# Experts of a fused attention and MoE kernel: the order of ScalarE, VectorE and GpSimd taken from the scheduler and given by lists

## Chip, cores and metric

The kernel runs on one core of a Trainium2 chip. The metric is the device time of one execution in microseconds (us). Times below in the profile are counted from the start of the profiled execution's span.

## What is computed

```
x  = attention(q, k, v)               # k and v averaged over 8 rows; 2304 tokens x 512
h  = x @ w_in;  x = (h * cos(h)) @ w_out          # 512 -> 2048 -> 512
P  = exp(x @ w_gate - max)                        # 2304 x 8
for _ in range(8):                                # Sinkhorn: rows, then columns
    P /= P.sum(1) + 1e-9;  P /= P.sum(0) + 1e-9;  P *= N / E
for e in range(8):
    out += P[:, e] * (relu(x @ w1[e]) @ w2[e])    # 512 -> 1024 -> 512
```

All is float32. Each operand of a product is split into a high half (float32r, rounded by ScalarE) and a low half (operand minus high half), and a product is three matmuls: high by high, high by low, low by high.

## The kernel before

The first third (to about 530 us) is attention and the cosine layer, and the change leaves it alone but for its end. The rest is the experts: 16 units (8 experts, two halves of 512 hidden columns each) for each of three pairs of 384-token blocks, 48 steps in all. The loop over `steps` (L990) writes one step after the other.

**First layer.** A step multiplies the pair's x by W1 in a Strassen-like scheme with seven products named P1, P5, P6, P2, P7, P3, P4, for two halves g of the columns: 14 blocks of six matmuls, the letters `a` in the order strings (L973 to L975). Px, py and pv are the PSUM banks that a half runs through. After P1, ScalarE copies px into py (L751), and P6, P7 and P4 add into py. After P5, ScalarE copies pv out (L754); VectorE adds it after P6 (L756) and after P7 (L768, or L794).

**Second layer.** Products of the step before run between the blocks. In the 16 steps of the first pair (plain steps) they are six groups `L` of 24 matmuls (L852), and VectorE adds each into the output (L839). In the other two pairs (Strassen steps) they are three groups `0`, `1`, `2` of four turns each (L869): a turn is two products of six matmuls, the last turn one. VectorE adds after the second turn (L888) and after the third (L892). Step 16, the first Strassen one, runs the plain second layer of step 15 (string `SWAP`).

**Preparation in the first pair.** In each plain step the weights of the next units are read raw, summed on GpSimd into Strassen's pieces (`combine`, L571), split (W1 in `split`, L93; W2 in `cut`, L631), and written to HBM for the later pairs (`w1c`, `w2c`). `w1_pieces` makes seven pieces; `w2_pieces` makes four blocks that the plain second layer uses and four sums that are only written out. Raw W2 tiles lie in `xh5` and `xl5`, raw W1 tiles in a pool of three. W1's halves lie in a pool of 19 tiles, W2's in `wp2` with 18. A tile comes free when its last reader is done, and for the pieces that includes the write to HBM.

**Preparation of x.** `x_pieces` makes seven pieces of the next pair's x in the last step of a pair (steps 15 and 31).

**Gate.** Logits, maximum, exponential and the eight Sinkhorn rounds run in steps 0 and 1. A round is a product with ones for the column sums (L555), then VectorE's scaling (`sinkhorn_columns`) and row and column sums (`sinkhorn_rows`).

**Order.** `tc.manual_schedule` (L976) holds TensorE alone to program order. ScalarE, VectorE, GpSimd and the DMA issues (all on SP's queue) are ordered by the framework's scheduler with its own model of time. `after[k]` is a list of calls that are made behind block k; what they issue on TensorE stands there, the rest is only traced from there.

Of the kernel before, what the change touches and what calls it, by code (L numbers as in the profile page):

```python
# [22 lines left out]
P = 128  # L23
# [35 lines left out]
def fused_kernel(ctx: ExitStack, tc: tile.TileContext, qT, kT, vT, v0, wa1, wb1, wa2, wb2, wg, out):  # L59
# [423 lines left out]
    def open_gate():  # L483

        gc = right(ctx, "gc", 1, reuse_waits="tile")
        gate["sk"] = right(ctx, "sk", 2, reuse_waits="tile")
        gate["tmp"] = right(ctx, "tmp", 3, reuse_waits="tile")
# [16 lines left out]
    def logits(j):  # L504

        sk = gate["sk"]
# [5 lines left out]
        lt = sk.tile([G2 + E, NB], F32, tag="lt", name="lt")  # L512
        nc.vector.tensor_copy(out=lt, in_=ps[:G2 + E, :])
        pq = gate["ps"][0].tile([P, TPB, E], F32, tag=gate["ps"][1], name="pq")
# [4 lines left out]
    def gate_max():  # L519

        sk, lg = gate["sk"], gate["lg"]
        m1 = sk.tile([P, 1], F32, tag="m1", name="m1")
        nc.vector.tensor_reduce(out=m1, in_=lg, op=ALU.max, axis=AX.XY)
        pm = gate["ps"][0].tile([P, P], F32, tag=gate["ps"][1], name="pm")
        nc.tensor.transpose(pm[:1, :], m1, ident)
        m2 = sk.tile([1, 1], F32, tag="m2", name="m2")
# [12 lines left out]
    def sinkhorn_rows():  # L539

        sk, pr = gate["sk"], gate["pr"]
        rw = sk.tile([P, NT, 1], F32, tag="rw", name="rw")
# [3 lines left out]
        nc.vector.tensor_tensor(out=pr, in0=pr, in1=rw.to_broadcast([P, NT, E]), op=ALU.mult)  # L546
        cs = sk.tile([P, E], F32, tag="cs", name="cs")
        nc.vector.tensor_reduce(out=cs, in_=pr.rearrange("p t e -> p e t"), op=ALU.add, axis=AX.X)
        gate["cs"] = cs

    def sinkhorn_columns():

        sk, pr = gate["sk"], gate["pr"]
        pc = gate["ps"][0].tile([P, E], F32, tag=gate["ps"][1], name="pc")
        nc.tensor.matmul(out=pc, lhsT=gate["ones"], rhs=gate["cs"], start=True, stop=True)  # L555
        cr = sk.tile([P, 1, E], F32, tag="cr", name="cr")
        nc.vector.tensor_scalar(
            out=cr[:, 0, :], in0=pc, scalar1=EPS, scalar2=float(E) / T, op0=ALU.add, op1=ALU.mult
        )
        nc.vector.reciprocal(out=cr, in_=cr)  # L560
        nc.vector.tensor_tensor(out=pr, in0=pr, in1=cr.to_broadcast([P, NT, E]), op=ALU.mult)
# [7 lines left out]

    def combine(out, x, y, op):  # L570
        nc.gpsimd.tensor_tensor(out=out, in0=x, in1=y, op=op)  # L571
        return out

    def w1_pieces(u):
# [10 lines left out]
        def piece(name):  # L585
            if name == "P1":
                what = a(1, 1)
            elif name == "P5":
                src["t"] = gate["tmp"].tile([P, FU], F32, tag="s", name="s")
                what = combine(src["t"], a(2, 1), a(2, 2), ALU.add)  # L590
            elif name == "P2":
                what = a(1, 2)
            elif name == "P6":
                what = combine(src["t"], src["t"], a(1, 1), ALU.subtract)
            elif name == "P7":
                what = combine(a(2, 1), a(1, 1), a(2, 1), ALU.subtract)
            elif name == "P3":
                what = combine(a(1, 2), a(1, 2), src["t"], ALU.subtract)
            else:
                what = a(2, 2)  # L600
            parts = split(what, nc.vector)
            for k, part in enumerate(parts):
                nc.sync.dma_start(out=w1c[u, ORDER.index(name), :, :, k, :],
                                  in_=part.bitcast(F32).rearrange("p (g n) -> p g n", g=2))
            w[name] = [[part[:, g * HD:(g + 1) * HD] for part in parts] for g in range(2)]

        return w, [lambda i=i: load(i) for i in range(2)], [lambda n=n: piece(n) for n in ORDER]
# [6 lines left out]
    def w2_pool(name):  # L614
        return wp if name in ("P1", "P5") else gate["wp2"]

    def w2_pieces(u):
# [3 lines left out]
        def load(h):  # L621
            src[h] = xp.tile([P, 2, DM], F32, tag=("xh5", "xl5")[h], name="raw2")
# [8 lines left out]
        def cut(what, pool, lo_engine):  # L631
            hi = pool.tile([P, FU], F32R, tag="w", name="vhi")
            lo = pool.tile([P, FU], F32R, tag="w", name="vlo")
            nc.scalar.activation(out=flat(hi), in_=what, func=AF.Copy)
            lo_engine.tensor_tensor(out=flat(lo), in0=what, in1=flat(hi).bitcast(F32), op=ALU.subtract)  # L635
            return hi, lo

        def keep(name, parts):
            for k, part in enumerate(parts):
                nc.sync.dma_start(out=w2c[u, ORDER.index(name), k], in_=part.bitcast(F32))  # L640

        def block(h, d):
            w[h - 1, d - 1] = cut(b(h, d), gate["wp2"], nc.gpsimd)
            name = {(1, 1): "P1", (2, 1): "P2", (2, 2): "P3"}.get((h, d))
            if name:
                keep(name, w[h - 1, d - 1])

        def tmp():
            return gate["tmp"].tile([P, 2, HD], F32, tag="s", name="t")

        def total(name):
            if name == "P5":
                src["t"] = combine(tmp(), b(1, 2), b(1, 1), ALU.subtract)
                what = src["t"]
            elif name == "P6":
                what = combine(src["t"], b(2, 2), src["t"], ALU.subtract)
            elif name == "P7":
                what = combine(tmp(), b(2, 2), b(1, 2), ALU.subtract)
            else:
                what = combine(src["t"], b(2, 1), src["t"], ALU.subtract)  # L660
            keep(name, cut(what, gate["wp2"], nc.vector))

        todo = [lambda h=h, d=d: block(h, d) for h, d in ((1, 1), (1, 2), (2, 1), (2, 2))]
        todo += [lambda n=n: total(n) for n in ("P5", "P6", "P7", "P4")]
        return w, [lambda h=h: load(h) for h in range(2)], todo

    def w2_cached(u, w, name):
        parts = []
        for k in range(2):
            t = w2_pool(name).tile([P, FU], F32R, tag="w", name="wc2")  # L670
# [6 lines left out]
    def x_pieces(pair):  # L677
# [13 lines left out]
        def piece(name):  # L691
# [4 lines left out]
            if name == "P1":  # L696
                what = b(1, 1)
            elif name == "P5":
                what = b(1, 1)
                nc.gpsimd.tensor_tensor(out=what, in0=b(1, 2), in1=b(1, 1), op=ALU.subtract)  # L700
            elif name == "P2":
                what = b(2, 1)
            elif name == "P6":
                what = b(1, 1)
                nc.gpsimd.tensor_tensor(out=what, in0=b(2, 2), in1=what, op=ALU.subtract)
            elif name == "P7":
                what = b(1, 2)
                nc.gpsimd.tensor_tensor(out=what, in0=b(2, 2), in1=what, op=ALU.subtract)
            elif name == "P3":
                what = b(2, 2)  # L710
            else:
                what = b(2, 1)
                nc.gpsimd.tensor_tensor(out=what, in0=what, in1=b(1, 1), op=ALU.subtract)
            t = xp.tile([P, 2, 2, NB], F32R, tag=XTAGS[name], name="xc")
            nc.scalar.activation(out=t[:, 0], in_=what, func=AF.Copy)
            nc.vector.tensor_tensor(out=t[:, 1], in0=what, in1=t[:, 0].bitcast(F32), op=ALU.subtract)  # L716
            x[name] = (t[:, 0], t[:, 1])

        return x, [lambda j=j: load(j) for j in (1, 2)], [lambda n=n: piece(n) for n in ORDER]

    def g_split(c, g):

        gh, gl = g_tiles(g)
        nc.scalar.activation(out=gh, in_=c, func=AF.Relu)
        nc.vector.scalar_tensor_tensor(
            out=gl, in0=c, scalar=0.0, in1=gh.bitcast(F32), op0=ALU.max, op1=ALU.subtract
        )
        return gh, gl
# [11 lines left out]
    def first_layer(weights, x, result):  # L740

        def sub(g, name, s):
            if name == "P1":
# [4 lines left out]
            ps = s[{"P1": "x", "P2": "x", "P5": "v", "P3": "v"}.get(name, "y")]  # L748
            x_product(ps, weights(name, g), x[name], name in ("P1", "P5"))
            if name == "P1":  # L750
                nc.scalar.activation(out=s["y"], in_=ps, func=AF.Copy)  # L751
            elif name == "P5":
                s["s5"] = cp.tile([P, NB], F32, tag="s5", name="s5", bufs=2)
                nc.scalar.activation(out=s["s5"], in_=ps, func=AF.Copy)  # L754
            elif name == "P6":
                nc.vector.tensor_tensor(out=s["v"], in0=ps, in1=s["s5"], op=ALU.add)  # L756
            else:
# [5 lines left out]
    def plain_result(gs):  # L763

        def result(g, name, ps, s):
            if name == "P7":
                c22 = cp.tile([P, NB], F32, tag="c22", name="c22")
                nc.vector.tensor_tensor(out=c22, in0=ps, in1=s["s5"], op=ALU.add)  # L768
                ps = c22
            h, j = {"P2": (0, 0), "P3": (0, 1), "P7": (1, 1), "P4": (1, 0)}[name]  # L770
            gs[2 * g + h, j] = g_split(ps, g)
# [3 lines left out]
    def strassen_result(pieces):  # L775
# [339 lines left out]
```

## Time and profile before

| | us |
|---|---|
| median of 3 runs | 2041.73 (2037.03 to 2042.55) |
| profiled execution | 2042.21 |
| its span | 2040.5 |
| first product of the experts (TensorE's first block of step 0) | 533.38 |

A row of the timeline names start, length, engine, line, what is written from what, count, and in brackets the idle time before and what ended it. In the windows each engine has its busy time and its number of instructions; then come TensorE's granted clock (1.00 is 2.4 GHz, 0.5 is 1.2 GHz), the mean busy share of the DMA engines and GB/s. A matmul's length in a row holds its latency; how fast they go is read from start to start.

### The profile page before, as it was taken

What the parts mean: (1) busy time and instruction counts of PE and PEld (TensorE: products, weight loads), DVE (VectorE), ACT (ScalarE), POOL (GpSimd) and SP (SyncE); (2) the same over time, 40 slices, a digit from 0 to 9 for tenths busy, and PEclk for the clock granted to TensorE, in tenths of its full rate; (3) what the DMA queues carried; (4) which work ended last, traced back from release to release, by engine and by line L of the source; (5) the groups of instructions that cost most, each with busy time, mean ns of one, the idle gap of its engine ahead of it and who ended that gap; (6) DMA issues with size and microseconds to landing.
All of it is one profiled execution on the core that took longest, in us unless ns stands there. A gap on an engine that the chain in (4) does not pass through costs nothing.

```text
span 2040.5 us, 36395 instructions
## 1 busy us (share of the span) xinstructions
PE 1966.0 (96%) x13220; PEld 1917.3 (94%) x13220; DVE 1380.9 (68%) x2279; ACT 992.3 (49%) x2133; POOL 770.8 (38%) x646
## 2 busy tenths in 40 slices
PE   6799999999889999999999999999999999999999
PEld 4689899999889999999999999999998999999999
DVE  8988776655786555556565676667667666666766
ACT  5676566655544444434443444444445444444443
POOL 7755644433344545454532221222223222222212
PEclk8899999999989999999999999999999999999999
DMA  7433331212688988888896776677677777667763
GB/s 254 144 123 126 113 119 53 84 52 77 228 292 296 304 276 301 270 293 292 278 316 222 266 263 229 240 275 250 225 256 250 241 261 275 230 235 269 258 230 121
DMA packets 257458, 453.32 MB, mean 222 GB/s; under 512 B 25568, under 2 KB 86752, under 8 KB 257280
## 3 DMA queue, kind: packets, MB, share of 16 engines
q1 hardware_dynamic: 257280, 451.01, 64.5%
q8 instruction: 104, 1.70, 0.3%
q14 instruction: 74, 0.61, 0.1%
HBM read 317.21 MB, written 133.69 MB: 221 GB/s over the span
## 4 chain that ended last, share of the span: by engine, by line
PE 76%; DVE 6%; DMA 6%; POOL 4%; ACT 3%; issue 3%; SPq 0%; ACTq 0%; POOLq 0%; DVEq 0%
PE pc L869 13%; PE py L736 13%; PE qc L869 10%; PE po L852 8%; PE px L736 8%; PE pv L736 8%; DMA w2c<-vhi 2%; PE ph L138 2%; PE po L137 2%; PE po L139 2%; PE ph L139 2%; PE po L138 2%; PE ph L137 2%; POOL vlo L635 1%; POOL t L571 1%
## 5 line engine op out<-in xcount | busy, mean ns | idle before, releaser
L869 PE MATMUL pc<-wc,gh 128*128 128x256 f32 x1536 | 284.1, 280 | 0.0
L571 POOL TENSOR_TENSOR sf<-spare 128x384 f32<-128x384 f32 x64 | 65.7, 1027 | 509.9 <-DVE spare L800 509.9
L869 PEld LDWEIGHTS pc<-wc,gh 128*128 128x128 f32 x1536 | 241.1, 188 | 0.0
L736 PE MATMUL py<-xc,wc 128*128 128x384 f32 x1152 | 236.1, 340 | 0.9 <-DVE c L794 0.6
L869 PE MATMUL pc<-wc,gl 128*128 128x256 f32 x768 | 215.6, 281 | 0.0
L869 PE MATMUL qc<-wc,gh 128*128 128x256 f32 x1152 | 214.1, 280 | 1.5 <-DVE pc L888 1.5
L736 PEld LDWEIGHTS py<-xc,wc 128*128 128x128 f32 x1152 | 196.6, 189 | 7.4 <-ACT py L751 5.1
L783 DVE TENSOR_TENSOR gl<-sf,gh 128x384 fp32r<-128x384 f32 x256 | 183.8, 758 | 10.8 <-ACT gh L782 7.3
L869 PEld LDWEIGHTS qc<-wc,gh 128*128 128x128 f32 x1152 | 185.9, 188 | 2.0 <-DVE pc L888 1.8
L869 PE MATMUL qc<-wc,gl 128*128 128x256 f32 x576 | 161.7, 281 | 0.0
L571 POOL TENSOR_TENSOR sf<-sf 128x384 f32<-128x384 f32 x64 | 80.8, 1262 | 210.9 <-DVE gl L783 210.9
L736 PE MATMUL pv<-xc,wc 128*128 128x384 f32 x768 | 156.2, 338 | 3.8 <-DVE xc L716 2.0
L736 PE MATMUL px<-xc,wc 128*128 128x384 f32 x768 | 154.3, 335 | 0.0
L852 PE MATMUL po<-vlo,gh 128*128 128x256 f32 x768 | 153.1, 281 | 0.0
L852 PE MATMUL po<-vhi,gl 128*128 128x256 f32 x768 | 152.8, 281 | 0.0
L852 PE MATMUL po<-vhi,gh 128*128 128x256 f32 x768 | 152.6, 281 | 0.0
L782 ACT ACTIVATE gh<-sf 128x384 fp32r<-128x384 f32 x256 | 119.9, 517 | 52.5 <-POOL sf L571 32.8
L869 PEld LDWEIGHTS pc<-wc,gl 128*128 128x128 f32 x768 | 145.1, 189 | 0.2 <-DVE gl L783 0.2
L137 PE MATMUL ph<-xh,whi 128*128 128x384 f32 x384 | 131.3, 346 | 5.9 <-DVE r L389 5.9
L736 PEld LDWEIGHTS pv<-xc,wc 128*128 128x128 f32 x768 | 131.0, 189 | 4.6 <-DVE xc L716 2.2
L138 PE MATMUL ph<-xl,whi 128*128 128x384 f32 x384 | 131.5, 343 | 0.7 <-DVE xl L370 0.7
L138 PE MATMUL po<-gl,whi 128*128 128x384 f32 x384 | 129.5, 338 | 0.8 <-POOL gl L392 0.8
(203 smaller groups left out, 5136.1 us busy)
## 6 DMA issues: line engine op xcount, KB each, us to landing
wc<-w1c SPq DMA_DIRECT2D x448, 256.0 KB, 5.2
wc<-w2c SPq DMA_DIRECT2D x448, 256.0 KB, 5.4
w1c<-whi SPq DMA_DIRECT2D x112, 256.0 KB, 3.4
w1c<-wlo SPq DMA_DIRECT2D x112, 256.0 KB, 3.3
w2c<-vhi SPq DMA_DIRECT2D x112, 256.0 KB, 3.9
w2c<-vlo SPq DMA_DIRECT2D x112, 256.0 KB, 4.3
raw<-wa SPq DMA_DIRECT2D x48, 512.0 KB, 6.2
raw<-wb SPq DMA_DIRECT2D x48, 512.0 KB, 4.6
```

The source lines that it names most:

```text
L137: nc.tensor.matmul(out=ps, lhsT=lh, rhs=rh, start=(i == 0), stop=False)
L138: nc.tensor.matmul(out=ps, lhsT=lh, rhs=rl, start=False, stop=False)
L139: nc.tensor.matmul(out=ps, lhsT=ll, rhs=rh, start=False, stop=(i == n - 1))
L571: nc.gpsimd.tensor_tensor(out=out, in0=x, in1=y, op=op)
L635: lo_engine.tensor_tensor(out=flat(lo), in0=what, in1=flat(hi).bitcast(F32), op=ALU.subtract)
L736: nc.tensor.matmul(out=ps, lhsT=l[:, k], rhs=r[:, c, :], start=(start and c + n == 0), stop=(c + n == 3), skip_group_check=True)
L782: nc.scalar.activation(out=hi, in_=t, func=AF.Copy)
L783: nc.vector.tensor_tensor(out=lo, in0=t, in1=hi.bitcast(F32), op=ALU.subtract)
L852: nc.tensor.matmul(out=po[:, d * HD:(d + 1) * HD], lhsT=l[:, r], rhs=w[f % 2, d][k][:, (f // 2) * HD:(f // 2 + 1) * HD], start=(f + n + d ...
L869: nc.tensor.matmul(out=ps, lhsT=l[:, r], rhs=m[:, k], start=(start and g + n == 0), stop=(g + n == 3), skip_group_check=True)
```

## The change

In the experts, ScalarE, VectorE and GpSimd too are held to program order:

```
-    with tc.manual_schedule(engines={mybir.EngineType.PE}):
+    E_ = mybir.EngineType
+    with tc.manual_schedule(engines={E_.PE, E_.Activation, E_.DVE, E_.Pool}):
         prime()
+        plan["on"] = True
```

The program order is made by three lists, one for each engine. `later` puts a call on a list, with the slot from which it may be made, its cost in us and a condition. After each block or group `tick` makes calls until the time of that block or group is used up. `until` makes calls ahead of time when a product needs what they give. A call made by `spent` is charged but was issued at once.

```
+    def later(engine, slots, us, run_it, at=0, ready=None, soon=False):
+        if plan["on"]:
+            k = sum(item[4] for item in plan[engine]) if soon else len(plan[engine])
+            plan[engine].insert(k, (max(plan["now"] + slots, at), us, run_it, ready, soon))
+        else:
+            run_it()
+    def tick(us):
+        for engine in "GAV":
+            left = min(plan["left"][engine] + us, max(us, 1.5))
+            k = 0
+            while k < len(plan[engine]) and left > 0:
+                slot, cost, run_it, ready, _ = plan[engine][k]
+                if slot > plan["now"] or (ready and not ready()):
+                    k += 1
+                    continue
+                plan[engine].pop(k)
+                run_it()
+                left -= cost
+            plan["left"][engine] = left
+        plan["now"] += 1
+    def until(done):
+        while not done():
+            ...      # makes the first ready call of each list
+    def parts_of(src, hi, lo, us, then, engine="V", slots=0, at=0):
+        def low():
+            e = nc.gpsimd if engine == "G" else nc.vector
+            e.tensor_tensor(out=lo(), in0=src, in1=high.bitcast(F32), op=ALU.subtract)
+            then()
+        def first():
+            nonlocal high
+            high = hi()
+            nc.scalar.activation(out=high, in_=src, func=AF.Copy)
+            later(engine, 1, us[1], low)
+        high = None
+        later("A", slots, us[0], first, at)
```

The ticks: 1.04 for a block, 2.8 for a plain group, 1.4 for a Strassen turn. Copies, ReLUs and sums that TensorE's next products need are issued at once; low halves, cuts, sums of pieces and gate operations go by the lists. `first_layer`, `plain_layer` and `strassen_layer` call `until` for the pieces that they read.

Engines that change: W1's low halves go from VectorE to GpSimd for units 0 to 2, and W2's low halves of the blocks with d = 2 from GpSimd to VectorE from unit 2 on; x's low halves of P7 and P3 go to GpSimd in the loop.

```
-            parts = split(what, nc.vector)
+            engine = "G" if u < 3 else "V"
+            parts_of(what, ..., (0.63, 1.4 if u < 3 else 0.8), done, engine, 0, at)
-            w[h - 1, d - 1] = cut(b(h, d), gate["wp2"], nc.gpsimd)
+            later("A", 0, 0.0, lambda: cut(..., "G" if d == 1 or u < 2 else "V"), 0, lambda: 1 in src)
+                engine = "G" if plan["on"] and name in ("P7", "P3") else "V"
```

Places in a plain step. W2's sums come ahead of its blocks, raw tiles are asked for from block 12 on, when all cuts of the pair in use are issued, and W2's last raw pair takes the raw W1 pool, so that x of pair 1 can be loaded at block 1 of step 15:

```
-                    put((0, 0), load)
-                    put((1, 3, 5, 7, 8, 9, 10, 11) if not last else (1, 2, 3, 4, 5, 6, 7, 8), todo)
-                    put(range(0, 14, 2), w_todo)
+                    for k, name in zip(((8, 9, 11, 13), (3, 4, 6, 9), (0, 1, 3, 9))[min(n, 2)], ("P5", "P7", "P6", "P4")):
+                        put(k, total, name)
+                    for k, (h, d) in zip((5, 7, 9, 11) if n else (5, 6, 7, 8), ((1, 1), (1, 2), (2, 1), (2, 2))):
+                        put(k, block, h, d)
+                        for k, name in ((3, "P5"), (4, "P6"), (7, "P7"), (8, "P3")):
+                            put(k, nw1[2], name)
+                        for k, name in enumerate(ORDER):
+                            put(5 + k, nw1[3], name)
+                                put(12, later, "A", 0, 0.0, lambda h=h, f=w1_next[1]: f(h), 0, lambda w=nw1[0]: len(w) == 7)
+                            put(12, later, "A", 0, 0.0, lambda h=h, f=w2_now[1]: f(h), 0, w2_read)
-                    put((8, 8) if pair == 0 else (2, 2), x_load)
+                        put(1, later, "A", 0, 0.0, f)
```

The gate's rounds stand three blocks apart in steps 1 and 2, and the output of expert 0 is scaled once the rounds are done (`first_scale`). The order strings change, and Strassen's pieces have 18 tiles of each half, where they had 20 low and 16 high. From step 17 on, the cuts of P7, P6, P2 and P3 of the first half wait for slot 16 of the step:

```
-    rest = [[lambda: logits(GRP[1][1])], [gate_max], [gate_exp, sinkhorn_rows], [], half, [], half]
-    rest += [half] * (SINKHORN_ITERS - 3) + [[sinkhorn_columns]]
+    rest = [{0: [late_logits], 2: [late_turn], 5: [max_turn], 8: [late_exp], 12: half},
+            {k: half for k in (1, 4, 7, 10, 13)}, {2: half, 5: [lambda: columns(False)]}]
-    GB = {"gl": 20, "gh": 16}
-    PLAIN = "aaLaaLaaLaaLaaLaaLaa"
+    GB = 18
+    PLAIN = "aaLaaLaaLaaaLaaLaaLa"
-    STRASSEN = "aaa0a1a01a01a01a2aa2a2a2aa"
+    STRASSEN = "aa0a1a0a1a0a1a0a2a1a2a2a2a"
+            free = start + 16 if g == 0 else 0
```

One pool of small gate tiles goes from 2 to 1 buffer, the pool of sums from 3 to 4, and the plain P3 of the first half takes its tile from the second half's pool.

## Rows read from the trace of the kernel before

**Rows 1.** The page: span, and each engine's busy us, share, instructions.
```profile
span 2040.5 us, 36395 instructions
...
PE 1966.0 (96%) x13220; PEld 1917.3 (94%) x13220; DVE 1380.9 (68%) x2279; ACT 992.3 (49%) x2133; POOL 770.8 (38%) x646
```
**Rows 2.** Windows: steps 0, 1, 2, 3 to 14, 16, 18, 31 to 32.
```profile
533.38:561.47 28.09, 21.71 (x106) 19.66 (x105) 18.11 (x36) 13.14 (x26) 15.09 (x11) 0.88 0.86 292
561.47:606.39 44.92, 36.10 (x241) 34.96 (x241) 39.01 (x85) 17.83 (x35) 19.56 (x15) 0.89 0.81 284
606.39:637.79 31.40, 31.40 (x229) 31.40 (x229) 23.37 (x35) 14.51 (x28) 18.01 (x14) 1.00 0.91 310
637.79:1030.89 393.10, 381.17 (x2737) 376.69 (x2737) 227.90 (x349) 170.24 (x324) 203.44 (x147) 1.00 0.86 288
1062.29:1099.08 36.79, 34.57 (x229) 32.80 (x229) 22.10 (x27) 12.21 (x25) 9.66 (x6) 0.95 0.83 301
1128.75:1158.30 29.55, 29.55 (x212) 29.40 (x211) 19.98 (x32) 13.48 (x33) 6.81 (x7) 1.00 0.70 242
1512.86:1578.26 65.40, 61.48 (x422) 60.07 (x422) 49.19 (x71) 32.42 (x72) 22.78 (x17) 0.97 0.71 239
```
**Rows 3.** Timeline of TensorE: first matmul of a P1 block, a group, a P5 block.
```profile
686.42 0.33 PE L736 MATMUL px<-xh,whi 128*128 128x384 f32 x1
...
687.46 0.40 PE L852 MATMUL po<-vhi,gh 128*128 128x256 f32 x2
...
690.26 0.51 PE L736 MATMUL pv<-xc,whi 128*128 128x384 f32 x2
```
**Rows 4.** Waits of TensorE in steps 0 and 1: total us, times, longest.
```profile
PE pc L555 <- DVE cs L548: 10.6, 4, 7.8
```
**Rows 5.** Waits of TensorE in steps 2 to 14.
```profile
PE py L736 <- ACT py L751: 10.3, 11, 1.7
```
**Rows 6.** Waits of TensorE from 1062 us to the end.
```profile
PE pv L736 <- DVE xc L716: 2.0, 1, 2.0
PE pv L736 <- ACT sf L802: 1.8, 1, 1.8
PE qc L869 <- DVE pc L888: 1.5, 1, 1.5
```
**Rows 7.** Timeline of ScalarE in step 4.
```profile
686.62 0.49 ACT L724 ACTIVATE gh<-py 128x384 fp32r<-128x384 f32 x1
691.33 0.63 ACT L634 ACTIVATE vhi<-t 128x512 fp32r<-128x512 f32 x1 [4.22 <-DMA w2c<-vhi]
691.87 0.61 ACT L96 ACTIVATE whi<-raw 128x512 fp32r<-128x512 f32 x1
692.38 0.47 ACT L751 ACTIVATE py<-px 128x384 f32<-128x384 f32 x1
```
**Rows 8.** Timeline of TensorE: the P6 block behind that copy.
```profile
692.91 0.44 PE L736 MATMUL py<-xc,whi 128*128 128x384 f32 x1 [1.44 <-ACT py L751]
```
**Rows 9.** Lines of GpSimd, steps 0 and 1: busy us, mean ns, idle before.
```profile
L635 POOL TENSOR_TENSOR vlo<-raw,vhi 128x512 fp32r<-128x512 f32 x10 | 14.4, 1462 | 9.1 <-ACT vhi L634 9.1
...
L571 POOL TENSOR_TENSOR t<-raw 128x512 f32<-128x512 f32 x2 | 2.6, 1311 | 2.2 <-DMA raw<-wb 2.2
```
**Rows 10.** Timeline of GpSimd at the loop's start.
```profile
537.66 1.28 POOL L571 TENSOR_TENSOR s<-raw 128x512 f32<-128x512 f32 x1 [20.36 <-DMA raw<-wa]
```
**Rows 11.** The page, DMA issues: count, KB each, median us to landing.
```profile
raw<-wb SPq DMA_DIRECT2D x48, 512.0 KB, 4.6
```
**Rows 12.** Timeline of VectorE in step 22.
```profile
1260.59 0.75 DVE L839 SCALAR_TENSOR_TENSOR acc<-pc,pr,acc 128x512 f32<-128x512 f32 x1 [0.27 <-PE pc L869]
1261.26 1.10 DVE L783 TENSOR_TENSOR gl<-spare,gh 128x384 fp32r<-128x384 f32 x1
...
1266.48 0.56 DVE L783 TENSOR_TENSOR gl<-c,gh 128x384 fp32r<-128x384 f32 x1 [1.28 <-ACT gh L782]
1266.95 2.31 DVE L783 TENSOR_TENSOR gl<-sf,gh 128x384 fp32r<-128x384 f32 x3
...
1270.40 0.43 DVE L888 TENSOR_TENSOR pc<-qc,t 128x256 f32<-128x256 f32 x1
```
**Rows 13.** Timeline of GpSimd in step 22.
```profile
1267.58 1.26 POOL L571 TENSOR_TENSOR sf<-sf 128x384 f32<-128x384 f32 x1 [5.63 <-DVE gl L783]
```
**Rows 14.** Lines of VectorE in steps 3 to 14: the low half of W1.
```profile
L97 DVE TENSOR_TENSOR wlo<-raw,whi 128x512 fp32r<-128x512 f32 x60 | 45.5, 759 | 3.2 <-PE px L736 2.0
```

More of the change, by code (lines that the diff above doesn't have):

```diff
@@ L583, in a, with total, t @@
             return src[i - 1][:, j - 1, :]
[L585 to L592, printed above, removed]
+        def total(name):
+            def t():
+                return gate["tmp"].tile([P, FU], F32, tag="s", name="s")
+            if name == "P5":
+                src["P5"] = combine(t(), a(2, 1), a(2, 2), ALU.add)
@@ L601, in piece @@
-            parts = split(what, nc.vector)
[L602 to L607, printed above, removed]
+                src["P3"] = combine(a(1, 2), a(1, 2), src["P6"], ALU.subtract)
@@ L629, in flat, with keep @@
             return t.rearrange("p (g n) -> p g n", g=2)
[L631 to L640, printed above, removed]
+        def keep(name, k, part):
+            nc.sync.dma_start(out=w2c[u, ORDER.index(name), k], in_=part.bitcast(F32))
@@ new lines, in cut, with tile_of, done @@
+        def cut(what, name, then, engine):
+            got = {}
+            def tile_of(k):
+                got[k] = gate["wp2"].tile([P, FU], F32R, tag="w", name=("vhi", "vlo")[k])
+                return flat(got[k])
+            def done():
+                if name:
+                    for k in range(2):
+                        keep(name, k, got[k])
+                then(got)
+            parts_of(what, lambda: tile_of(0), lambda: tile_of(1), (0.65, 1.4 if engine == "G" else 0.8), done, engine)
@@ L742, in sub @@
         def sub(g, name, s):
+            until(lambda: name in x and weights(name, g) is not None)
+            until(lambda: not any(reads[b] for b in {"P1": "xy", "P5": "v"}.get(name, "")))
             if name == "P1":
@@ L845, in group @@
         def group(j, i):
+            until(lambda: len(w) == 4 and all((f, j) in gs for f in range(FC)))
             po = psp.tile([P, DM], F32, tag="p", name="po")
@@ L863, in mm @@
             r = slice(i * P, (i + 1) * P)
+            until(lambda: all((name, g) in pieces for g in range(2)))
             wh, wl = w[name]
@@ L1026, in fused_kernel @@
-                    nxt = strassen_layer(pair, u, pieces, w2, acc2, own)
-                x_next = x_op
+                    first = first_layer(lambda name, g, n=n: ring[n, name, g], x_op, strassen_result(pieces, start if n > NU else start - 99))
+                    own = {2: ((psx, "x"), (psy, "y"))} if n == len(steps) - 1 else None
+                    nxt = strassen_layer(pair, u, pieces, w2, acc2, own)
+                if n == UE:
+                    for j in range(2):
+                        for i in range(TPB):
+                            put(13, later, "V", 0, 0.65, lambda j=j, i=i, a=acc2: first_scale(j, i, a), 0,
+                                lambda: gate.get("done"))
```

411 lines of the change are left out of this document (261 added, 150 removed).

## The prediction, made before the changed kernel ran

> **What bounds the kernel now.** I read the busy shares first. TensorE is busy 96% of the span and no other engine is above 68% [rows 1], so time can come only from TensorE's gaps and slow stretches. The second view is the windows by expert step [rows 2]. Step 2 is a clean plain step. Its 31.40 us equal 14 first-layer blocks of 1.04 and 6 second-layer groups of 2.80, both read as distances between matmul starts [rows 3]: 14.56 + 16.80 = 31.36. Step 18 is a clean Strassen step of 29.55. Against these two the other windows show what is lost:
>
> - Steps 0 and 1 take 28.09 and 44.92, where 14 blocks (14.6) and a plain step (31.4) would do: 27.0 over. Their counts of 106 and 241 hold 22 and 13 matmuls beyond the 84 and 228 of the products. These 35 small ones are the gate's own; at no more than 0.174 each (1.04 / 6) they explain 6 at most, and I put them at 5. So 22 is lost.
> - Steps 3 to 14 take 393.10, twelve clean ones 376.8: 16.3 lost.
> - Step 16, the passage to Strassen: 36.79 against 31.4: 5.4 lost.
> - Steps 31 and 32, where the last pair's x is prepared: 65.40 against 59.1: 6.3 lost.
>
> Together 50.0 us. Some of it is half speed: the granted clock is 0.88 and 0.89 in the first two windows, which hold TensorE's longest idle stretch, and 1.00 in the clean ones [rows 2].
>
> The third view is TensorE's waits, which name the culprits. In steps 0 and 1 it waited 10.6 for VectorE's column sums, 7.8 of that at once [rows 4]. In steps 2 to 14 it waited 10.3 for ScalarE's copy of px into py, 11 times [rows 5]. After that come single waits of 2.0, 1.8 and 1.5 at the two passages [rows 6]. The fourth view, ScalarE's order of time, shows why the copy is late [rows 7]. It sits behind a cut of W2 whose buffer was still being written to HBM: ScalarE stood 4.22 there, did two cuts, copied at 692.38, and TensorE's P6 began at 692.91 after 1.44 idle [rows 8]. Its input had been ready since 687.46.
>
> **The change, part by part.** No matmul goes or comes. ScalarE, VectorE and GpSimd lose the scheduler's order and run in the order in which the lists emit. Sums are made on the profiled execution's own 2042.2 us (span 2040.5 and 1.7 around it), which is 0.5 above the median of 2041.73.
>
> *Gate rounds (part of steps 0 and 1).* They go from every second block of steps 0 and 1 to every third of steps 1 and 2. Between two column products there are then three blocks and one or two groups, 5.9 to 8.7 us, in place of two blocks and at most one group. A round is some eight small VectorE operations, and 7.8 was lost when they came late. These waits go. What is late next is GpSimd.
>
> *Low halves of W1 on GpSimd for units 0 to 2 (steps 0 to 2).* Each step cuts seven W1 pieces and four W2 blocks and makes eight sums. In steps 0 and 1 the 11 low halves cost 1.46 each on GpSimd and the 8 sums 1.31 [rows 9]: 16.1 + 10.5 = 26.6 us. Unit 0's seven low halves fall ahead of the loop, where GpSimd was idle for 20.36 [rows 10], and cost nothing; without that cover they would cost up to 2. Step 0's work starts when its raw tile lands at 537.7 and ends at 564.3 if nothing holds it. Step 1 would start near 551.5 (533.4 + 14.6 + some 3.5 of the gate). Its first group, two blocks on, needs the last W2 block, which lies eight items before the end, at 553: just in time. The second 26.6 cannot start whole at 564.3, since W2's next raw pair reuses the tiles just read: a last cut of 1.5 and a landing of 4.6 [rows 11] put it at 570. GpSimd ends between 590.9 (W1's share fills the hole) and 597. Step 2's first group (551.5 + 32.9 + 2.1 = 586.5) needs the W2 block that is last but one in that order: 589.4 to 595.5. So TensorE waits 3 to 9 there. VectorE's delays behind so busy a GpSimd add 1 to 8. Of the 22 lost I keep 9 (ends 4 and 17): 13 gained.
>
> Here a row speaks against the change. Three VectorE low halves in a row took 2.31 while one GpSimd product of 1.26 ran beside them [rows 12, 13]; with GpSimd idle the next one followed 0.47 after the first (1266.48 to 1266.95), so among the three one stood about as long as the product. The Trainium skill, SBUF — State Buffer, section "Who interferes with whom", has the rule: a VectorE instruction with two SBUF inputs and a GpSimd instruction that reads SBUF share a port and the later one stands until the first is done. The trace agrees with it. By that rule moving low halves to GpSimd frees VectorE of less than their length; it is a rival below.
>
> *W2's sums ahead of its blocks, raw tiles asked for after the last cut (steps 3 to 14).* The four sums move from blocks 8 to 11 to blocks 0, 1, 3 and 9. At block 0 only the eight W2 tiles of the unit in use are held, of 18. The sums' six tiles find room, and their writes have landed before the blocks need it. So the wait in front of the copy goes [rows 7]. The plain order also puts a group between P5 and P6 of the second half, which gives that copy 2.80 + 1.04 in place of 1.04. Two low halves per step go from GpSimd to VectorE, at 0.76 each [rows 14]; VectorE is busy 228 of 393 there and takes it. New is that ScalarE's first cut of a step stands behind a GpSimd sum, which stands behind a raw tile asked for near the last group of the step before: 4.6 to land, 1.3 for the sum. That is about 6 us, and the cut stands some 6 to 9 us after the request. Queued behind it are the ReLU of P2 and later the copy of P1, which TensorE needs some 9 us on. Five us of lateness stay hidden. Of 16.3 I keep 2.5 (ends 0 and 8): 13.8 gained.
>
> *Step 16.* The x tiles of pair 1 are asked for at block 1 of step 15 in place of 8, since W2's last raw pair moves to another pool, and two of their low halves go to GpSimd. TensorE's 2.0 wait for VectorE's xc goes. The memory that the Strassen tiles reuse still has to be freed at the same point. Of 5.4 I keep 2.4: 3.0 gained.
>
> *Steps 31 and 32.* The same seven pieces, loaded a block earlier, with VectorE at 49.19 of 65.40 busy. Two of seven low halves leave it and the rest come by budget. Of 6.3 I keep 3.0 (ends 0 and 8): 3.3 gained.
>
> *Strassen order (steps 17 to 47).* No row shows a loss here now, so the edit can only cost. Groups 0 and 1 get more room between their turns. Group 2's second and third turn have one block between them as before: VectorE must add (L888) between P6 and the next turn's P7. In the new order P6's block ends 4.2 us before that P7 (a last turn 0.70, a block 1.04, a turn 1.40, a block 1.04). VectorE has the P6 add, up to four low halves that were held for that slot, and one accumulation ahead of the add: 0.47 + 4 x 0.47 + 0.67 + 0.43 = 3.45 alone (starts in [rows 12]). 0.7 is left. Bounds: 0 per step, and 1.7 (three low halves held, each by a GpSimd product). GpSimd is busy 6.81 of 29.55 there [rows 2] and due elsewhere, so I take the near end: 1 in all.
>
> Sum: 13 + 13.8 + 3.0 + 3.3 - 1 = 32.1, and 2042.2 - 32.1 = 2010.
>
> **The rivals.**
>
> - *GpSimd is the bound at the start.* It ends batch two at 597 or later, VectorE's two-input operations (four W2 low halves, two of c, ten in gate rounds) wait for its products, and a low clock follows. Speaks for it: 26.6 per step, [rows 12, 13]. Against: it was busy only 15 and 20 us in these two windows. Gains of steps 0 to 2 fall from 13 to 1: 2022.
> - *Nearly all gaps close.* 47 of the 50.0 go: 1995. For: every wait named above has a new cover. Against: 26.6 us of GpSimd work per step.
> - *Slower: VectorE comes late to group 2's turn.* If three of the four low halves take 1.29 in place of 0.47, the add is 2.46 - 0.7 = 1.7 late in each of 31 steps: 53 us, so 2062. It decides from 33.1 / 31 = 1.1 per step. For: an order fixed on paper cannot step around a blocked instruction. Against: GpSimd's products of the first half are done by then.
> - *The lists move the waits without shortening them.* ScalarE stands behind GpSimd sums in place of HBM writes, 1.1 per plain step again, and the start gives 5: about 2037. For: [rows 5] is a wait of this sort now. Against: the slack of 5 us worked out above.
>
> **How the numbers follow.** Forecast 0.48 (own range 2000 to 2020), overloaded start 0.16, nearly all gone 0.13, no change 0.10, slower 0.13. A difference of 0.3% (6 us) is about what can be told from none. Faster: 0.48 + 0.16 + 0.13 + 0.02 of the fourth = 0.79. Same 0.08, slower 0.13. The range 1993 to 2045 takes in all but the slower rival and a little beyond the floor.
>
> **What would show it.** Right: steps 3 to 14 at 31.4 to 31.7 each with no wait of py for its copy; steps 0 to 2 in 90 to 95 us in place of 104.4; step 16 under 35; steps 17 to 30 still at 29.55. Wrong: a Strassen step over 29.7, with TensorE waiting for L888's add; GpSimd busy past 95% in step 1 and TensorE waiting in step 2; ScalarE idle before its first W2 cut for longer than 5 us.

## The result and the profile after

The changed kernel takes 2012.3 us (median of four runs, 2011.89 to 2015.24) against 2041.65 before (four runs): a ratio of 0.9864 with an interval of 0.9846 to 0.9881. The forecast was 2010, so total and sign came out. That the total came so close is luck in part: two terms of the sum were too high by 8.9 together and the others too low by 6.9 (table below). The page of the changed kernel first: span, then each engine's busy us, share and instructions.

```profile
span 2010.4 us, 36447 instructions
...
PE 1955.4 (97%) x13220; PEld 1917.9 (95%) x13220; DVE 1354.3 (67%) x2282; ACT 988.4 (49%) x2133; POOL 765.2 (38%) x643
```
No matmul went and the other engines did almost the same work as in [rows 1]. The span fell by 30.1 and TensorE's busy time by 10.6 (1966.0 to 1955.4). The matmul count is the same, so they took less each; steps 0 and 1 show a granted clock of 0.96 and 0.98 below, 0.88 and 0.89 in [rows 2]. The other 19.5 is idle time. Now the windows, with the columns of [rows 2]: steps 0, 1, 2, the three together, 3 to 14, 15 and 16 together, 18, 31 and 32.

```profile
531.70:553.17 21.47, 19.16 (x104) 18.05 (x103) 10.74 (x26) 11.29 (x22) 13.16 (x11) 0.96 0.85 289
553.17:589.87 36.70, 34.09 (x239) 33.35 (x239) 31.49 (x59) 12.95 (x26) 28.55 (x22) 0.98 0.86 290
589.87:628.28 38.41, 34.09 (x236) 33.50 (x234) 29.35 (x53) 17.15 (x34) 23.36 (x18) 0.96 0.87 296
531.70:628.28 96.58, 87.34 (x575) 84.90 (x573) 71.58 (x136) 41.38 (x82) 65.06 (x49) 0.96 0.86 292
628.28:1005.99 377.71, 377.37 (x2737) 376.82 (x2737) 265.30 (x380) 166.94 (x324) 169.57 (x120) 1.00 0.89 303
1005.99:1074.88 68.89, 65.43 (x457) 64.39 (x457) 39.50 (x52) 23.68 (x47) 24.24 (x14) 0.98 0.91 314
1104.36:1133.84 29.48, 29.48 (x211) 29.48 (x211) 18.32 (x32) 13.53 (x33) 6.61 (x7) 1.00 0.74 252
1487.60:1549.41 61.81, 60.09 (x421) 59.00 (x421) 45.43 (x69) 32.06 (x72) 25.88 (x19) 1.00 0.74 255
```
Set against the starts of the steps before (us; a gain is positive):

| stage | before | after | gained | forecast |
|---|---|---|---|---|
| up to the loop | 533.4 | 531.7 | 1.7 | 0 |
| steps 0 to 2 | 104.4 | 96.6 | 7.8 | 13 |
| steps 3 to 14 | 393.1 | 377.7 | 15.4 | 13.8 |
| steps 15, 16 | 68.2 | 68.9 | -0.7 | 3.0 (step 16) |
| steps 17 to 30, 33 to 46 | 827.5 | 825.4 | 2.0 | -1 |
| steps 31, 32 | 65.4 | 61.8 | 3.6 | 3.3 |
| from step 47 on | 48.6 | 48.3 | 0.3 | 0 |

They sum to 30.1, the difference of the spans. TensorE's waits in the changed kernel: steps 0 to 2, then steps 3 to 14, then from 1006 us on (total us, times, longest).

```profile
PE po L1025 <- POOL vlo L646: 2.3, 1, 2.3
PE pv L860 <- DVE gl L840: 2.0, 1, 2.0
PE pc L570 <- DVE cs L562: 1.7, 2, 1.4
...
PE pv L860 <- DVE gl L840: 0.2, 1, 0.2
...
PE pv L860 <- DVE gl L840: 2.8, 1, 2.8
PE pc L1043 <- DVE gl L646: 1.1, 1, 1.1
```
The wait for column sums, 10.6 in [rows 4], is 1.7. The twelve plain steps hold one wait of 0.2 where [rows 5] had 10.3. What was forecast to take its place on ScalarE, a first cut behind GpSimd's sum, is there, and hidden. ScalarE's waits in steps 3 to 14:

```profile
ACT vhi L652 <- POOL t L639: 94.2, 36, 7.2
```
ScalarE stands there up to 7.2 and TensorE waits for none of it: the cover of the lead worked out in the prediction held, though it had named a wait of more than 5 there as a sign of being wrong. VectorE's busy time in these steps rose by 37.4 (227.9 to 265.3), twice the 18.2 of the 24 low halves that moved to it at 0.76 each; that is hidden too.

**Step 2.** It grew from 31.40 to 38.41, of which 4.3 is TensorE's idle time. The timelines of GpSimd, then of ScalarE:

```profile
572.40 1.46 POOL L639 TENSOR_TENSOR s<-raw 128x512 f32<-128x512 f32 x1 [3.87 <-DMA raw<-wa]
...
588.82 1.62 POOL L639 TENSOR_TENSOR raw<-raw,s 128x512 f32<-128x512 f32 x1
...
596.46 1.33 POOL L646 TENSOR_TENSOR vlo<-raw,vhi 128x512 fp32r<-128x512 f32 x1
```
```profile
590.47 0.63 ACT L652 ACTIVATE whi<-raw 128x512 fp32r<-128x512 f32 x1 [7.17 <-POOL raw L639]
...
592.05 0.47 ACT L850 ACTIVATE gh<-pv 128x384 fp32r<-128x384 f32 x1
```
GpSimd's second batch began at 572.40 (570 forecast) and ran nearly without a gap; the W2 low half that a group needs was done at 597.8 (589.4 to 595.5 forecast). ScalarE stood 7.17 for one of its sums, and the ReLU of pv (the result of P3 in the step before), queued behind two more cuts, came only at 592.05. These are two of the three long waits above.

**The passage.** Step 16 is 36.57 with one long wait, 2.8. VectorE, GpSimd and TensorE there, and ahead of them the same VectorE operation some 20 us earlier:

```profile
1017.56 0.68 DVE L646 TENSOR_TENSOR vlo<-t,vhi 128x512 fp32r<-128x512 f32 x1
...
1037.03 1.86 DVE L646 TENSOR_TENSOR vlo<-t,vhi 128x512 fp32r<-128x512 f32 x1
1038.82 2.30 DVE L646 TENSOR_TENSOR vlo<-raw,vhi 128x512 fp32r<-128x512 f32 x1
1041.05 0.74 DVE L1011 SCALAR_TENSOR_TENSOR acc<-po,pr,acc 128x512 f32<-128x512 f32 x1
1041.71 0.54 DVE L840 SCALAR_TENSOR_TENSOR gl<-pv,gh 128x384 fp32r<-128x384 f32 x1
```
```profile
1035.79 4.79 POOL L806 TENSOR_TENSOR x1r<-x1r 128x768 f32<-128x768 f32 x2
1040.53 2.27 POOL L646 TENSOR_TENSOR xc<-x1r,xc 128x768 fp32r<-128x768 f32 x1
```
```profile
1042.30 0.85 PE L860 MATMUL pv<-xc,wc 128*128 128x384 f32 x3 [2.78 <-DVE gl L840]
```
Two low halves of W2 that take 0.68 alone took 1.86 and 2.30 beside GpSimd's x sums; the second (from raw) is one of those that the change moved from GpSimd to VectorE. In the held order the low half of pv stood behind them, and the matmul that reuses pv came 2.78 late. The wait is not its whole price. The window in which it ends:

```profile
1042.00:1046.00 4.00, 3.70 (x16) 3.70 (x17) 4.00 (x4) 0.00 (x0) 4.00 (x3) 0.62 0.94 310
```
After those 2.78 idle TensorE's granted clock is 0.62 on the mean of these four us, much of them at the lower level of 1.2 GHz, and they hold 16 matmuls where the next four hold 32.

### The profile page after: what moved, and what is told of

Its sections match the earlier page's. It is cut to its first block, busy times and chain, and to the rows that moved or that the text cites. A ratio compares the mean times of both kernels' runs of the same rounds, so it can differ in the third digit from the quotient of the medians.

```text
span 2010.4 us, 36447 instructions
## 1 busy us (share of the span) xinstructions
PE 1955.4 (97%) x13220; PEld 1917.9 (95%) x13220; DVE 1354.3 (67%) x2282; ACT 988.4 (49%) x2133; POOL 765.2 (38%) x643
## 4 chain that ended last, share of the span: by engine, by line
PE 67%; DVE 2%; issue 1%; DMA 1%; POOL 1%; ACT 1%; SPq 0%; DVEq 0%; POOLq 0%; ACTq 0%
PE py L860 14%; PE pc L1043 13%; PE po L1025 11%; PE qc L1043 10%; PE pv L860 9%; PE px L860 9%; DMA raw<-wb 1%; DVE gl L646 1%; POOL t L639 0%; DVE vlo L646 0%; DMA w2c<-vhi 0%; POOL vlo L646 0%; DVE gl L840 0%; POOL wlo L646 0%; DVE acc L1011 0%
## 5 line engine op out<-in xcount | busy, mean ns | idle before, releaser
L1043 PEld LDWEIGHTS qc<-wc,gh 128*128 128x128 f32 x1152 | 191.6, 188 | 0.9 <-DVE pc L1062 0.6
L646 DVE TENSOR_TENSOR gl<-sf,gh 128x384 fp32r<-128x384 f32 x256 | 148.5, 619 | 9.8 <-ACT gh L652 9.8
L860 PEld LDWEIGHTS px<-xc,wc 128*128 128x128 f32 x768 | 130.7, 188 | 0.0
L886 DVE TENSOR_TENSOR pv<-py,s 128x384 f32<-128x384 f32 x96 | 54.2, 564 | 113.5 <-ACT gh L652 87.9
```

The lines of the kernel that those rows point to most:

```text
L646: e.tensor_tensor(out=lo(), in0=src, in1=high.bitcast(F32), op=ALU.subtract)
L860: nc.tensor.matmul(out=ps, lhsT=l[:, k], rhs=r[:, c, :], start=(start and c + n == 0), stop=(c + n == 3), skip_group_check=True)
L1043: nc.tensor.matmul(out=ps, lhsT=l[:, r], rhs=m[:, k], start=(start and g + n == 0), stop=(g + n == 3), skip_group_check=True)
```

## The experiments

Each edit is to the changed kernel, but for one to the kernel before. The ratio is to the kernel before.

| edit | us | ratio (95%) | steps 0 to 3 | 3 to 14 | 15, 16 | 31, 32 |
|---|---|---|---|---|---|---|
| the change | 2012.3 | 0.9864 (0.9846 to 0.9881) | 128.9 | 377.7 | 68.9 | 61.8 |
| hold TensorE alone | 2014.66 | 0.9874 (0.9859 to 0.9888) | 127.7 | 384.1 | 64.2 | 62.8 |
| old W2 places | 2012.4 | 0.9859 (0.9845 to 0.9874) | 126.1 | 377.5 | 68.7 | 61.8 |
| old plain order | 2017.42 | 0.9883 (0.9868 to 0.9898) | 128.0 | 379.8 | 73.3 | 61.8 |
| both old | 2038.14 | 0.9987 (0.9978 to 0.9997) | 129.8 | 396.9 | 74.9 | 61.8 |
| before, new plain order | 2068.81 | 1.0134 (1.0110 to 1.0159) | 146.3 | 417.6 | 65.9 | 64.5 |
| W1 lows on VectorE | 2016.19 | 0.9872 (0.9852 to 0.9892) | 128.9 | 379.6 | 68.8 | 61.8 |
| gate two apart | 2029.66 | 0.9938 (0.9914 to 0.9961) | 141.7 | 380.8 | 68.8 | 61.8 |
| gate four apart | 2010.09 | 0.9854 (0.9839 to 0.9868) | 124.8 | 377.2 | 68.0 | 61.8 |
| x lows on VectorE | 2013.53 | 0.9862 (0.9842 to 0.9882) | 129.6 | 379.9 | 68.9 | 60.8 |
| last W2 early | 2010.53 | 0.9862 (0.9846 to 0.9879) | 129.2 | 378.2 | 65.5 | 61.8 |
| no hold to slot 16 | 2019.65 | 0.9904 (0.9889 to 0.9919) | 129.3 | 379.4 | 68.9 | 63.2 |
| three together | 2004.96 | 0.9819 (0.9800 to 0.9838) | 125.1 | 377.7 | 65.0 | 60.8 |

Step 3 stands in two columns. "Steps 0 to 3" is 136.8 in the kernel before; the others stand in the table above. Each stage is read from one profiled execution. In the kernels whose edit lies outside steps 3 to 14 that column still runs from 377.2 to 380.8, nearly all of it in step 3 (31.8 to 35.4).

**Places or holding.** Does the gain in the plain steps come from the new places in the lists, or from holding three more engines to them?

```
-    with tc.manual_schedule(engines={E_.PE, E_.Activation, E_.DVE, E_.Pool}):
+    with tc.manual_schedule(engines={E_.PE}):
```


> The changed kernel with TensorE alone held to program order; lists, places and order strings stay, ScalarE, VectorE and GpSimd go back to the scheduler. If the places (W2's sums first, a group between P5 and P6, gate rounds apart) make the gain, steps 3 to 14 stay within 377 to 382 us and the whole within 2005 to 2020. If holding the three engines to an order makes it, the scheduler puts waits back: steps 3 to 14 at 386 to 393, the passages as before, the whole 2025 to 2042.

The window of steps 3 to 14, then TensorE's largest wait in it:

```profile
627.22:1011.29 384.07, 379.66 (x2738) 377.12 (x2737) 256.25 (x375) 166.00 (x323) 170.31 (x121) 1.00 0.90 304
```
```profile
PE pv L860 <- DVE gl L840: 3.3, 4, 1.6
```
384.1 lies between the two ranges; the whole, 2014.66, lies in the first. All the rest of the change under the scheduler's order gives 9.0 of the 15.4 (393.1 - 384.1), the holding the other 6.4. At the passage holding loses 4.7 (68.9 against 64.2). Over the whole span holding the three engines gains 1.6 of the 30.1 (2012.0 against 2010.4), and the intervals of the two ratios overlap. So its worth in total is not told from nothing: nearly all of the gain comes with the lists, their places, the engines chosen and the order strings.

**Which of the two covers.** The prediction named two: W2's sums ahead of its blocks, and a group between P5 and P6 of the second half. Each was put back alone, then both.

```
-(0, 1, 3, 9))[min(n, 2)], ("P5", "P7", "P6", "P4")
+(0, 1, 3, 9) if last else (8, 9, 10, 11))[min(n, 2)], ("P5", "P7", "P6", "P4")
-zip((5, 7, 9, 11) if n else (5, 6, 7, 8), ...
+zip((1, 3, 5, 7) if 2 <= n < NU - 1 else (5, 7, 9, 11) if n else (5, 6, 7, 8), ...
```


> The changed kernel with W2's blocks at 1, 3, 5, 7 and its sums at 8 to 11 again in steps 2 to 14; the new plain order stays. Theory (buffers): ScalarE waits again for W2's tiles to be written to HBM, over 30 us in steps 3 to 14, but the group between P5 and P6 hides most of the late copy: 378 to 386 us. Rival (room): these places cost nothing, 377.7 as in the changed kernel, waits of ScalarE for writes under 10.

```
-    PLAIN = "aaLaaLaaLaaaLaaLaaLa"
+    PLAIN = "aaLaaLaaLaaLaaLaaLaa"
```


> The changed kernel with the old plain order string, so that P6 follows P5 of the second half at once; W2's new places stay. Theory (buffers): with no wait for writes the copy comes in time in the gap of 1.04 us or nearly: steps 3 to 14 at 378 to 382, whole 2012 to 2018. Rival (room): the copy has 1.04 us and VectorE's low half of P4 ahead of it, so about 1.2 us per step come back: 389 to 393, whole 2024 to 2030.

> The changed kernel with both old: W2's places (steps 2 to 14) and the plain order string. If these two make the gain of steps 3 to 14 and the fixed order adds nothing, 389 to 395 us there, whole 2023 to 2032. If holding the engines to an order makes it, 377 to 382, whole 2012 to 2018.

With one cover gone, the sums' place or the order string, steps 3 to 14 stay at 377.5 and 379.8:

```profile
626.98:1004.47 377.49, 377.35 (x2737) 376.67 (x2737) 256.88 (x378) 164.91 (x324) 168.29 (x120) 1.00 0.87 301
627.64:1007.46 379.82, 378.99 (x2737) 376.32 (x2737) 263.80 (x380) 163.61 (x324) 168.65 (x120) 1.00 0.87 300
```
With both gone they take 396.9, above both ranges given for it. So in the held order one is enough and neither alone is the cause. (At the passage the old string costs 4.4 as well, 73.3 against 68.9.) With W2's sums late, ScalarE stands for the writes to HBM again, for a time between the two figures expected, and TensorE waits for none of it:

```profile
ACT vhi L652 <- DMA w2c<-vhi: 20.6, 9, 3.7
```
With both gone: the window, TensorE's only wait in it, and VectorE and TensorE at one such wait.

```profile
629.83:1026.77 396.94, 380.24 (x2737) 376.40 (x2737) 245.40 (x379) 163.63 (x325) 163.00 (x120) 1.00 0.84 287
```
```profile
PE pv L860 <- DVE gl L840: 16.7, 12, 1.4
```
```profile
728.68 0.74 DVE L1011 SCALAR_TENSOR_TENSOR acc<-po,pr,acc 128x512 f32<-128x512 f32 x1
729.34 1.28 DVE L646 TENSOR_TENSOR wlo<-raw,whi 128x512 fp32r<-128x512 f32 x2
730.54 0.55 DVE L840 SCALAR_TENSOR_TENSOR gl<-c,gh 128x384 fp32r<-128x384 f32 x1
731.01 0.55 DVE L840 SCALAR_TENSOR_TENSOR gl<-pv,gh 128x384 fp32r<-128x384 f32 x1
```
```profile
731.61 0.61 PE L860 MATMUL pv<-xc,whi 128*128 128x384 f32 x2 [1.40 <-DVE gl L840]
```
It is another wait than in [rows 5]: not ScalarE's copy, but pv's low half on VectorE, which in the held order stands behind two W1 low halves (1.28), once in each of twelve steps. Each time it is at block 2 of the step, P5, which reuses the pv that P3, block 13 of the step before, has filled. In the old string P3, P4, P1 and P5 follow one another there; the new one has a group between P3 and P4. So the cover that counts is read as that group, and not the one between P5 and P6; the two were not tried apart. The copy's wait of [rows 5] does not come back in any of the three kernels. A held order without its covers loses 20.1 over 376.8 clean, more than the 16.3 of the kernel before.

**The plain order alone, in the kernel before.** PLAIN there takes the new string, nothing else.

> The kernel before with nothing changed but the plain order string (a group between P5 and P6 of the second half). If room for the copy is cover enough under the scheduler too, TensorE's wait for ScalarE's copy goes: steps 3 to 14 at 377 to 382 us in place of 393.1, the whole 2026 to 2031. If the new places of W2's cuts are needed, the copy comes late by more than one group: 389 to 394 there, the whole 2037 to 2043.

```profile
641.75:1059.33 417.58, 395.28 (x2737) 382.09 (x2737) 228.00 (x348) 167.45 (x324) 197.28 (x147) 1.00 0.80 271
```
```profile
PE po L852 <- ACT gh L724: 8.2, 10, 1.8
PE pv L736 <- DVE gl L725: 6.7, 11, 1.2
PE py L736 <- ACT py L751: 6.4, 9, 1.5
```
Both theories missed: it is slower, by 24.5 in these steps. The wait for the copy is cut only to 6.4, and two others of 8.2 and 6.7 join it. TensorE's idle time explains 10.4 of the 24.5 (22.3 against 11.9); the other 14.1 is longer busy time at a granted clock of 1.00, and why stays open. The string is a cover only with the other changes around it; which of them it needs was not taken apart further.

**Is GpSimd the bound of steps 0 to 2?** The W1 low halves of units 1 and 2 go back to VectorE.

```
-            engine = "G" if u < 3 else "V"
+            engine = "G" if u < 1 else "V"
```


> The changed kernel with W1's low halves of units 1 and 2 on VectorE (14 of 1.3 us leave GpSimd). Theory (GpSimd too full at the start): step 1 falls from 36.7 to 33 to 36 and step 2 from 38.4 to 32 to 34, steps 0 to 2 from 96.6 to 88 to 92, the whole 2004 to 2008. Rival (VectorE's gate rounds are what is late): VectorE gets 10 us more in a stretch where it is busy 61 of 75; steps 0 to 2 at 97 to 102, the whole 2013 to 2018.

Steps 0 to 2, and TensorE's two largest waits:

```profile
535.17:630.83 95.66, 86.27 (x574) 83.27 (x573) 76.62 (x148) 41.70 (x82) 48.88 (x35) 0.98 0.84 284
```
```profile
PE pc L570 <- DVE cs L562: 4.8, 3, 2.3
PE py L860 <- DVE c L904: 2.3, 2, 1.3
```
GpSimd is 16.2 less busy (65.06 to 48.88), VectorE 5.0 more, and the three steps are 0.9 shorter. The length lies between the two ranges. The wait for GpSimd's low half goes, that for the column sums comes back: what leaves one engine is waited for on the other, and neither engine's load alone is shown to set these steps. (Of the 4.3 by which its span is longer, 3.5 is its loop start, 535.2.)

**How far apart the gate's rounds stand.** Two blocks apart, all in step 1; then four apart, over steps 1 and 2.

```
-            {k: half for k in (1, 4, 7, 10, 13)}, {2: half, 5: [lambda: columns(False)]}]
+            {k: half for k in (0, 2, 4, 6, 8, 10)} | {12: [lambda: columns(False)]}]
```


> The changed kernel with seven gate rounds two blocks apart (blocks 0 to 12 of step 1), none in step 2. If the distance of three blocks makes the gain of the start, TensorE waits for the column sums again, 3 to 8 us in step 1, and the whole is 2014 to 2020. If it does not matter (two blocks and a group are long enough for a round), waits stay under 2 us, step 2 gets shorter by what VectorE does less there, and the whole is 2009 to 2013.

```
-            {k: half for k in (1, 4, 7, 10, 13)}, {2: half, 5: [lambda: columns(False)]}]
+            {k: half for k in (2, 6, 10)}, {0: half, 4: half, 8: half, 12: [lambda: columns(False)]}]
```


> The changed kernel with the gate's rounds four blocks apart, three in step 1 and four in step 2. Theory: two apart cost 13 more in steps 0 to 3 than three apart because VectorE, held by GpSimd, needs longer for a round than two blocks; at four apart the waits for column sums (1.7 in steps 0 to 2) go and VectorE is freer for the low halves: steps 0 to 3 at 122 to 127 us in place of 128.9. Rival: what is left there is GpSimd's and VectorE's common load, which the distance does not change: 127.5 to 131.

Two apart, TensorE's wait for column sums up to 606 us; four apart, the window of steps 0 to 3:

```profile
PE pc L570 <- DVE cs L562: 14.5, 8, 3.4
```
```profile
531.10:655.94 124.84, 117.27 (x802) 114.86 (x801) 95.98 (x174) 55.03 (x109) 80.75 (x59) 0.99 0.90 305
```
Two apart costs 12.8 over steps 0 to 3, more than expected; four apart gains 4.0, as much as expected but not for the reason given, since the waits for column sums go from 1.7 only to 1.4. TensorE's idle time is 2.0 less, most of it in the wait for pv in step 2 (2.0 to 0.5), and the granted clock is 0.99 against 0.97. VectorE and GpSimd are as busy with four as with three (95.98 and 80.75 against 96.27 and 79.60): the same work, farther apart. The profiled execution is the shortest of the four; their median is 2.2 under the change, and the last experiment repeats the gain in these steps.

**The passage: who holds VectorE?** One theory named the two x low halves on GpSimd, the other the late place of W2's last blocks.

```
-                engine = "G" if plan["on"] and name in ("P7", "P3") else "V"
+                engine = "V"
```


> The changed kernel with x's low halves of P7 and P3 on VectorE again in the loop. Theory (VectorE held by GpSimd at the passage): GpSimd loses two low halves of 2.3 to 2.6 us in steps 15 and 16, VectorE's low halves of 1.9 to 2.6 get shorter, steps 15 and 16 fall from 68.9 to 65 to 68 us. Rival (VectorE's own load): it takes two of 0.9 to 1.7 us more, steps 15 and 16 at 69 to 71, and steps 31 and 32 above 61.8.

```
-(0, 1, 3, 9))[min(n, 2)], ("P5", "P7", "P6", "P4")
+(0, 1, 3, 9) if not last else (0, 1, 2, 5))[min(n, 2)], ("P5", "P7", "P6", "P4")
-zip((5, 7, 9, 11) if n else (5, 6, 7, 8), ...
+zip((2, 3, 4, 6) if last else (5, 7, 9, 11) if n else (5, 6, 7, 8), ...
```


> The changed kernel with W2's cuts of step 15 placed earlier: sums at blocks 0, 1, 2, 5 and blocks at 2, 3, 4, 6, where it has 0, 1, 3, 9 and 5, 7, 9, 11. Theory: at the passage to Strassen VectorE stands with the last two W2 low halves behind GpSimd's x sums, and the low half of P3 that TensorE waits 2.8 for stands behind them; with W2 done before x begins, steps 15 and 16 fall from 68.9 to 63 to 66 us, the whole 2007 to 2010. Rival: x's own chain (high, low, sum, seven times) is too long for the time left, and W2 moved earlier only fills another place: 68 to 70, the whole 2011 to 2014.

With the x low halves on VectorE, TensorE's largest wait there; with W2 early, the same, then the window of steps 15 and 16:

```profile
PE pv L860 <- DVE gl L840: 2.8, 1, 2.8
```
```profile
PE pv L860 <- DVE gl L840: 0.9, 1, 0.9
```
```profile
1007.42:1072.92 65.50, 64.04 (x458) 63.03 (x457) 35.62 (x52) 24.09 (x47) 23.18 (x14) 1.00 0.96 331
```
The first theory falls: with those low halves gone from GpSimd the wait is the same 2.8, since the x sums (L806) still stand beside W2's last low halves. Moving W2's last blocks ahead of them gives 3.4 (68.9 to 65.5), as expected there (the whole, 2010.53, is just above its range): step 16 falls by 4.2 (36.57 to 32.39), 2.8 of waiting and 1.4 of busy time at a clock now 1.00. Step 15 grows by 0.8 (32.33 to 33.11), and the wait of 0.9 is in it. In steps 31 and 32 the x low halves are 1.0 better off on VectorE, where more than 61.8 was expected.

**Holding cuts to slot 16 in the Strassen steps.** The prediction's slower rival lives on the slot for which low halves are held; here nothing is held.

```
-            free = start + 16 if g == 0 else 0
+            free = 0
```


> The changed kernel without the hold of the first half's cuts to slot 16 in the Strassen steps. Theory: with an order that cannot step around a blocked instruction, ScalarE reaches those cuts when no tile of the 18 is free and stands until group 2 of the step before has run, and the ReLUs and copies behind it come late: 0.5 to 3 us in each of 30 steps, 2027 to 2100. Rival: tiles come free in time or ScalarE has room to wait: steps stay at 29.48 to 29.6, the whole 2010 to 2016.

One Strassen step, and a wait of ScalarE over steps of that kind that the changed kernel doesn't list:

```profile
1163.00:1192.60 29.60, 29.60 (x212) 29.54 (x211) 18.23 (x33) 13.38 (x32) 6.62 (x6) 1.00 0.75 249
```
```profile
ACT gh L652 <- PE pc L1043: 37.6, 12, 3.1
```
A step is 29.63 on the mean against 29.48, 4 us over 28 steps. That is under the theory's 0.5 per step and just above the rival's 29.6, and the whole, 2019.65, lies between the two ranges. Steps 31 and 32 lose 1.4 more. Step 3 is 1.5 longer too (33.81 against 32.29), but it lies ahead of the edit and moves as much in other kernels. No single wait of TensorE shows the 0.15, so through which wait it comes is open.

**Three together.** The early W2 of the last plain step, the gate four apart, and the x low halves on VectorE for the last pair alone (`if plan["on"] and pair == 1 and name in ("P7", "P3")`).

> The changed kernel with W2's cuts of step 15 earlier, gate rounds four blocks apart, and the low halves of P7 and P3 of the last pair's x on VectorE. If the three are apart in time and add: 3.4 + 4.0 + 1.0 us off the changed kernel's span, 2003 to 2006. If the start only shifts from run to run of the scheduler's order ahead of the loop (the loop begins between 531.4 and 535.2 in the kernels so far), the sum is hidden by that: 2006 to 2010.

```profile
span 2003.2 us, 36458 instructions
...
PE 1952.9 (97%) x13220; PEld 1915.3 (96%) x13220; DVE 1349.8 (67%) x2284; ACT 987.3 (49%) x2133; POOL 758.5 (38%) x641
```
2004.96: 7.3 under the change, 36.5 under the kernel before as measured beside it (2041.44). The parts add: 3.7 in steps 0 to 3, 3.9 at the passage and 1.0 in steps 31 and 32, less 0.5 in steps 4 to 14 and 1.1 at the loop's start (532.8).

## Why the prediction came out, and which terms did not

- **Gate and start (13 forecast, 7.8 measured).** The step "of the 22 lost I keep 9" was mis-sized: the three steps keep 14.2 (96.58 less 14.6 + 31.4 + 31.4 + 5), of which 9.2 is idle time. That the gate's wait would go was right (10.6 to 1.7), and that GpSimd would be late in step 2 too, but the latest block came 2.3 past the late end given. The reason given, GpSimd's load, is not shown to be it: with 14 low halves moved off, the length changed by 0.9, as VectorE was waited for instead. The spacing of the rounds does set the length: 12.8 worse at two, 4.0 better at four.
- **The port row [rows 12, 13].** It was weighed as a cost of steps 0 to 2 and decided at another place, the passage: 0.68 alone, 1.86 and 2.30 beside GpSimd's 4.79. The Trainium skill, SBUF — State Buffer, section "Who interferes with whom", has it that such a pair of instructions hold one shared port in turn; the trace agrees.
- **Plain steps (13.8 forecast, 15.4 measured).** The size was right, and the new wait behind GpSimd's sum was there and hidden. The mechanism is only in part borne out. The copy's wait went, and with the new places and TensorE alone held it is 0.3; but in the held order it stays away with the sums' old place and the old string together, so neither of the two reasons given is needed for it there. 6.4 of the gain needs the held order. The prediction did not see that in a fixed order the next to be late is pv's low half on VectorE, which either of the two covers.
- **Step 16 (3.0 forecast, -0.7 for steps 15 and 16).** This step failed. The 2.0 wait for xc [rows 6] went, but in step 15 W2's blocks had moved from blocks 1 to 4 to blocks 5 to 11 and its last sum from 8 to 9, onto GpSimd's x sums, and a wait of 2.8 took its place. Step 16 gained 0.2 (36.79 to 36.57), and step 15 lost 0.9 (31.40 to 32.33). The prediction counted what the move frees and not what it is moved beside.
- **Steps 31 and 32 (3.3 forecast, 3.6 measured).** Right.
- **Strassen steps (-1 forecast, +2.0 measured).** Right in that they stay at 29.55 or under; the slower rival's mechanism did not come about. Why a step is 0.07 shorter stays open; it is 29.48 with TensorE alone held too, so the holding is not the cause.
- **Up to the loop (0 forecast, 1.7 measured).** Over the changed kernels the loop starts between 531.1 and 535.2, in some where the edit lies behind it. What orders the work there was not taken apart.
- **The signs.** Steps 4 to 14 came at 31.4 each (step 3 at 32.3) and steps 17 to 30 at 29.48, as said. Steps 0 to 2 (96.6, not 90 to 95) and step 16 (36.57, not under 35) missed. TensorE did wait in step 2, but GpSimd was busy 78% of step 1 (28.55 of 36.70), not 95%.

## What to carry to other kernels

Measure a held order apart from what is held: here the holding gained 6.4 in the plain steps, lost 4.7 at the passage and was worth 1.6 of 30.1 in all. A fixed order on several engines pays when each wait has a cover and costs when one has none: here either of two covers made the plain steps clean, and without both the held order was as slow as the kernel before. When work is moved, read the engine's neighbour at its new place: W2's last blocks cost a wait of 2.8 us beside the x sums and 1.4 more at a lower clock. For a chain of small dependent operations between matmuls, distance between its rounds was worth more than which engine is relieved.

## What the runs showed of the hardware that was not expected

A tensor-tensor of VectorE beside GpSimd's took up to 3.4 times its time alone (2.30 against 0.68), and the operation behind it, which reads PSUM and took its usual 0.54, started late behind them. In the plain steps such delays cost TensorE nothing; here they cost it 2.78: what stands behind the pair decides the price. With 14 low halves moved to it in steps 0 to 2, VectorE spent 13.3 more on W1's low halves (19.7 for 21 against 6.4 for 7), 0.95 each and not 0.76 [rows 14], yet its busy time rose by only 5.0. Three of the gate's operations (L554, L560 and L578, eight of each in both kernels) took 14.0 in place of 18.1 beside a quieter GpSimd, and the steps stayed as long all the same.
